# Storing each output tile of a fused attention and maxout kernel with one transfer of 128 rows instead of two of 64

## The chip, the cores and the metric

The kernel runs on one core of a Trainium2 chip. The metric is device time in microseconds (us) of the whole program, as a median of several runs. A profile of one execution gives a span, from the first to the last instruction, about 2 us below the run's time. Ratios are the mean time of one kernel's fast runs over the mean of the other's in the same rounds, so they are not quite the ratio of the medians that are quoted.

The engines, by what they do in this kernel (instructions on the page of the kernel before): TensorE (PE, 4316) multiplies matrices, VectorE (DVE, 521) and ScalarE (ACT, 289) do elementwise work, GpSimd (POOL, 260) copies and starts loads, SyncE (SP) issues transfers, the only thing that its timeline shows. The bytes are moved by DMA engines, of which the page counts sixteen. A run counts as slow when it is over 1.5% above the fastest of the same kernel, otherwise as fast; only fast runs are compared.

## The reference

```python
# q, k, v: (8, 12, 448, 64) float32; w1, w2, w3, w_out: (768, 768) float32
scores = q @ k.T / sqrt(64);  m = max(scores);  e = exp(scores - m)
attn   = (e / (sum(e) + exp(-m) + 1e-9)) @ v           # per batch and head
x      = attn, heads side by side                      # (3584, 768)
h      = maximum(maximum(x @ w1, x @ w2), x @ w3)
out    = h @ w_out                                     # (3584, 768) float32
```

## The kernel before

Attention runs group by group (four heads of a batch), and the projections of batches already finished fill TensorE's time in between. Queries stand in an unusual order inside the kernel: a batch has seven blocks of 64 columns, and column x of block n is output row 7 x + order[n]. An output tile takes two blocks (128 columns of `hT`), so its 128 rows are two sets of 64 rows; inside a set the rows are seven apart. In the code and the profiles `stp` are the scores, `e` their exponentials, `xn` and `xT` the attention's result and its transpose, `p_i` one projection, `hT` the maximum of the three, `op_ps` the last product and `o_sb` its copy that is stored. Each set is stored by one transfer:

```python
    NW = DM // 2
    order = (0, 2, 4, 6, 1, 3, 5)

    def out_piece(bp, t, c, w, queues):
        # ... six matmuls into op_ps[:, 0:w], lhsT = 128 columns of hT ...
        nc.vector.tensor_scalar(out=o_sb[:, c : c + w], in0=op_ps[:, 0:w], ...)
        if queues is None:
            return
        for half in range(2):
            n = 2 * t + half
            b = 2 * bp + n // T
            rows = out[b * S : (b + 1) * S].rearrange("(p t) m -> t p m", t=T)[order[n % T]]
            queues[half].dma_start(
                out=rows[:, outs[1] : c + w], in_=o_sb[half * HP : half * HP + HP, outs[1] : c + w]
            )
        outs[1] = c + w
```

SP's queue also carries the transposes that feed TensorE: `QT` and `KT` for the scores of a group two iterations ahead, and `xT` for the projections:

```python
    def transpose_dma(i):
        for dst, nm, o in ((QT[i], "q", 4), (KT[i], "k", 0)):
            nc.sync.dma_start_transpose(...)     # [cut]

    def x_transpose_dma(i):
        nc.sync.dma_start_transpose(out=..., in_=...)     # [cut] xT <- xn
```

The softmax here doesn't subtract the row's maximum and nothing guards it: scores larger than these inputs give would overflow.

Of the kernel before, what the change touches and what calls it, by code (L numbers as in the profile page):

```python
# [21 lines left out]
def kernel(  # L22
# [13 lines left out]
    B, H, S, D = q.shape  # L36
    NTOK, DM = out.shape
    DFF = moe_w1.shape[1]
    NDC = DM // 128
    NFC = DFF // 128  # L40
# [5 lines left out]
    HP = 64  # L46
    T = S // HP
# [86 lines left out]
    for nm, src, eng in (("k", k, nc.sync), ("q", q, nc.scalar)):  # L134
# [10 lines left out]
            outs=[],  # L145
# [333 lines left out]
    outs = {}  # L479
# [23 lines left out]
    NW = DM // 2  # L503
    order = (0, 2, 4, 6, 1, 3, 5)

    def out_piece(bp, t, c, w, queues):

        if c == 0:
            outs[0] = out_pool.tile([128, DM], FP32, tag="o_sb", name="o_sb")
            outs[1] = 0  # L510
        o_sb = outs[0]
        op_ps = ps_b.tile([128, 512], FP32, tag="b", name="op_ps")
        for fc in range(NFC):
            nc.tensor.matmul(  # L514
                out=op_ps[:, 0:w],
                lhsT=hT[bp][:, fc, ts(t, 128)],
                rhs=wout_sb[:, fc, c : c + w],
                start=(fc == 0),
                stop=(fc == NFC - 1),
            )  # L520
        nc.vector.tensor_scalar(  # L521
            out=o_sb[:, c : c + w], in0=op_ps[:, 0:w], scalar1=1.0 / LAMBDA, scalar2=None,
            op0=ALU.mult,
        )
        if queues is None:
            return
        for half in range(2):
            n = 2 * t + half
            b = 2 * bp + n // T
            rows = out[b * S : (b + 1) * S].rearrange("(p t) m -> t p m", t=T)[order[n % T]]  # L530
            queues[half].dma_start(
                out=rows[:, outs[1] : c + w], in_=o_sb[half * HP : half * HP + HP, outs[1] : c + w]
            )
        outs[1] = c + w


    UP = NDC * (S + 6)
    pieces = []
# [7 lines left out]
    def add_out(b):  # L546
        sy, sc = nc.sync, nc.scalar
        for t in range(0, 3) if b % 2 == 0 else range(3, 7):
            cuts = [(0, NW, None), (NW, NW, (sy, sy))]
            if b == B - 1 and t == 6:  # L550
                cuts = [(0, NW, (sy, sy)), (NW, 256, (sc, sc)), (NW + 256, 128, (sy, sc))]
            for c, w, queues in cuts:
                pieces.append((out_piece, (b // 2, t, c, w, queues), NFC * (w + 6)))

    def add_batch(b):
        add_up(b, 0, S, [(i, fc) for fc in range(NFC) for i in range(3)])
        add_out(b)
# [120 lines left out]
    for i in range(3, NI):  # L678
# [6 lines left out]
        for vi, units in enumerate(visits):  # L685
            n = 3 * i + vi
# [16 lines left out]
            if vi == 2 and first:  # L703
                x_transpose_pe(i - 1, "E")
                fill(per / 2)
                prep_v(i, DV)
                for w, cols in ((0, (0, NE)), (1, (0, NE)), (2, (NE, NO)), (2, (0, NE))):
                    add_up(0, *cols, [(w, f) for f in (0, 2, 4)])
                add_out(0)
                per = share(n)  # L710
# [59 lines left out]
```

## Time and profile before

| | before |
|---|---|
| median | 339.16 us (338.11 to 339.39, 4 runs) |
| span of the profile | 336.9 us |
| TensorE busy | 326.1 us, 97% |
| last VectorE work to the end | 331.9 to 336.9: 5.0 us |
| transfers for the stores | 60 (57 from SP, 3 from ACT), 11.01 MB |

The prediction below shows and reads the main lines. Two more are needed later: the count of DMA packets on the page, and the line of the waits for GpSimd's copies of QT (engine, line, whom it waited for, total us, times, longest).

```profile
DMA packets 84815, 46.46 MB, mean 138 GB/s; under 512 B 53280, under 2 KB 81312, under 8 KB 84768
...
POOL QT L249 <- DMA QT<-ld_q: 69.2, 11, 10.0
```

The packet count includes packets of 4 bytes, called semaphore packets here: 2656 of them on the queues of SP and ScalarE. A store of this kernel leaves sixteen (pair_one below has 30 stores fewer and exactly 480 such packets fewer), so the sixty stores make 960. I read it as one for each DMA engine that carries the store; the number of store packets in flight at a time, which in this kernel is sixteen for longer than any other number (10.3 of 53.5 us), agrees. This count will tell how many engines a transfer used.

### The profile page before, as it was taken

To read this page: it belongs to the slowest core of one execution; us is meant where nothing else is said; L and a number is where in the kernel's file an instruction comes from. 1 tells how busy PE (TensorE), PEld (TensorE's weight loads), DVE (VectorE), ACT (ScalarE), POOL (GpSimd) and SP (SyncE) were. 2 spreads that over 40 slices of the span, in tenths; PEclk is the share of its full clock that TensorE was granted. 3 is DMA by queue.
4 is the path that set the end of the run, shared out by engine and by line. 5 is a ranking of instruction groups with operands and counts; after the bars stand their busy time and mean duration, and the time that the engine had idled before them with its cause. 6 is when DMAs were issued, how large, how long until landed. Compare 5 with 4: busy or idle time off the path is not lost.

```text
span 336.9 us, 10248 instructions
## 1 busy us (share of the span) xinstructions
PE 326.1 (97%) x4316; PEld 195.9 (58%) x4316; DVE 199.9 (59%) x521; ACT 183.1 (54%) x289; POOL 146.7 (44%) x260
## 2 busy tenths in 40 slices
PE   7899999999999999999999999999999999999993
PEld 3668788866556655565546646555556555565552
DVE  4556675566566556556656556556556556575552
ACT  4768856655665755676556655666565665420000
POOL 8596578880671539170854328351754000000000
PEclk9999999999999999999999999999999999999999
DMA  8999999799799999969996999989990730124016
GB/s 141 197 200 207 203 205 191 128 161 191 109 108 132 171 234 145 124 96 190 177 156 81 114 259 120 150 99 220 186 149 18 164 89 2 31 47 129 0 33 157
DMA packets 84815, 46.46 MB, mean 138 GB/s; under 512 B 53280, under 2 KB 81312, under 8 KB 84768
## 3 DMA queue, kind: packets, MB, share of 16 engines
q0 software_dynamic: 29120, 21.80, 48.6%
q1 hardware_dynamic: 55264, 23.60, 41.3%
q8 instruction: 34, 0.56, 0.7%
q10 hardware_dynamic: 384, 0.39, 0.4%
q14 instruction: 13, 0.11, 0.1%
HBM read 44.04 MB, written 11.01 MB: 163 GB/s over the span
## 4 chain that ended last, share of the span: by engine, by line
PE 87%; DMA 5%; ACT 2%; DVE 2%; issue 1%; POOL 1%; POOLq 0%; ACTq 0%
PE p_i L490 48%; PE op_ps L514 14%; PE stp L304 11%; PE avp L388 9%; DMA xT<-xn 3%; ACT e L324 2%; DMA ld_q<-in_q_dram 2%; PE avp L344 2%; PE avp L361 1%; DVE xn L404 1%; PE trT L229 1%; DVE QT L190 1%; PE xtp L463 0%; ACT QT L188 0%; DVE rb L401 0%
## 5 line engine op out<-in xcount | busy, mean ns | idle before, releaser
L324 ACT ACTIVATE e<-stp 128x896 f16<-128x896 f32 (+4 forms) x171 | 143.9, 901 | 60.3 <-PE stp L304 60.1
L490 PE MATMUL p_i<-xT,w 128*128 128x448 f16 (+2 forms) x972 | 173.1, 332 | 0.5 <-DMA xT<-xn 0.3
L490 PEld LDWEIGHTS <-w 128*128 128x128 f16 x972 | 90.2, 98 | 69.1 <-issue 6.0
L249 POOL COPY QT<-QT 64x384 f16<-64x384 f16 (+1 forms) x84 | 46.9, 558 | 93.9 <-DMA QT<-ld_q 69.2
L501 DVE TENSOR_TENSOR hT<-hT,p_i 128x448 f16<-128x448 f16 (+2 forms) x96 | 59.7, 622 | 35.7 <-PE p_i L490 35.6
L514 PE MATMUL op_ps<-w,hT 128*128 128x384 f16 (+2 forms) x342 | 58.5, 323 | 0.0
L304 PE MATMUL stp<-QT,KT 64*64 64x448 f16 (+2 forms) x756 | 48.1, 338 | 2.6 <-ACT e L324 0.9
L499 DVE CAST hT<-p_i 128x448 f16<-128x448 f32 (+2 forms) x48 | 30.0, 625 | 25.2 <-PE p_i L490 25.2
L514 PEld LDWEIGHTS <-hT 128*128 128x128 f16 x342 | 32.0, 98 | 22.4 <-issue 2.0
L424 ACT ACTIVATE xn<-end,rl 64x64 f16<-64x64 f32 x72 | 24.9, 346 | 34.5 <-DVE rl L421 34.1
L521 DVE TENSOR_SCALAR o_sb<-op_ps 128x384 f32<-128x384 f32 (+2 forms) x57 | 31.2, 547 | 17.4 <-PE op_ps L514 16.8
L388 PE MATMUL avp<-vx,e 128*128 128x65 f16 x936 | 38.6, 194 | 0.0
L388 PEld LDWEIGHTS <-e 128*128 128x128 f16 x936 | 32.1, 97 | 2.3
L304 PEld LDWEIGHTS <-KT 64*64 64x64 f16 x756 | 15.8, 105 | 26.8 <-issue 23.9
L398 DVE TENSOR_SCALAR rb<-avp 128x6 f32<-128x6 f32 (+2 forms) x54 | 8.8, 164 | 36.8 <-PE avp L388 36.8
L404 DVE TENSOR_TENSOR xn<-avp,rb 128x384 f16<-128x384 f32 (+2 forms) x54 | 29.3, 543 | 1.8
L433 POOL COPY vx<-ld_v 128x768 f16<-128x768 f16 x21 | 17.2, 820 | 6.8 <-issue 4.2
L344 PEld LDWEIGHTS <-e 64*64 64x64 f16 x624 | 13.7, 107 | 8.1 <-issue 1.7
L102 POOL DMA_DIRECT2D ld_q<-in_q_dram x24 | 17.4, 723 | 2.3 <-DMA w<-in_moe_w_dram 1.1
L102 POOL DMA_DIRECT2D ld_k<-in_k_dram x24 | 17.3, 722 | 2.1 <-DMA w<-in_moe_w_out_dram 1.1
L414 ACT ACTIVATE end<-avp 128x65 f32<-128x65 f32 x36 | 8.2, 227 | 17.1 <-PE p_i L490 12.4
L115 POOL DMA_DIRECT2D ld_v<-in_v_dram x24 | 15.2, 634 | 2.6 <-DMA w<-in_moe_w_dram 1.3
(52 smaller groups left out, 162.1 us busy)
## 6 DMA issues: line engine op xcount, KB each, us to landing
out_dram<-o_sb SPq DMA_DIRECT2D x54, 192.0 KB, 4.0
ld_v<-in_v_dram POOLq DMA_DIRECT2D x48, 128.0 KB, 5.1
ld_k<-in_k_dram POOLq DMA_DIRECT2D x23, 224.0 KB, 6.6
ld_q<-in_q_dram POOLq DMA_DIRECT2D x23, 224.0 KB, 7.5
w<-in_moe_w_dram POOLq DMA_DIRECT2D x9, 384.0 KB, 9.2
w<-in_moe_w_out_dram POOLq DMA_DIRECT2D x3, 384.0 KB, 8.5
xT<-xn SPq DMA_TRANSPOSE x18, 4.8
QT<-ld_q SPq DMA_TRANSPOSE x17, 7.3
```

The costliest lines, as they stand in the source:

```text
L102: nc.gpsimd.dma_start(out=tiles[nm][:, 1 : NP * T + 1].rearrange("x (r t) d -> x r (t d)", r=NP)[:, p0:p1], in_=src[:, p0:p1],)
L249: eng.tensor_copy(out=t[d0 : d0 + HP, o * 128 : (o + n) * 128], in_=t[s0 : s0 + HP, a * 128 : (a + n) * 128],)
L304: nc.tensor.matmul(out=stp[half * HP : half * HP + HP, par, j * qn : (j + 1) * qn], lhsT=k_block(i, pr, h2, x[half]), rhs=q_cols(i, pr, h2 ...
L324: nc.scalar.activation(out=dst, in_=src, func=AF.Exp, scale=scale)
L388: nc.tensor.matmul(out=ps[:, hh, j * D1 : (j + 1) * D1], lhsT=eF[:, o : o + 128], rhs=vx[:, 2 * pr + hh, (x[0]), 0:D1], start=False, stop= ...
L404: nc.vector.tensor_tensor(out=xn[i][:, pr, ws[0] : ws[0] + nw].rearrange("p j h d -> p h j d"), in0=acc[:, :, :, 0:D], in1=rb.unsqueeze(3) ...
L424: nc.scalar.activation(out=xn[i][0:HP, pr, 3, hh], in_=end[h, 0:D], func=AF.Copy, scale=rl[h])
L490: nc.tensor.matmul(out=p_i[:, j * qn : (j + 1) * qn], lhsT=w_sb[i][:, dc, ts(fc, 128)], rhs=xT[b][:, dc, q0 : q0 + qn], start=(dc == 0), s ...
L499: nc.vector.tensor_copy(out=dst, in_=src)
L501: nc.vector.tensor_tensor(out=dst, in0=dst, in1=src, op=ALU.max)
L514: nc.tensor.matmul(out=op_ps[:, 0:w], lhsT=hT[bp][:, fc, ts(t, 128)], rhs=wout_sb[:, fc, c : c + w], start=(fc == 0), stop=(fc == NFC - 1),)
L521: nc.vector.tensor_scalar(out=o_sb[:, c : c + w], in0=op_ps[:, 0:w], scalar1=1.0 / LAMBDA, scalar2=None, op0=ALU.mult,)
```

## The change

The intent is fewer transfers: both sets of rows of a tile in one. It builds a pattern of three dimensions in DRAM by hand: 2 sets, 64 rows, the columns. Where the second set comes before the first in DRAM (t = 5, four tiles of 28) two transfers stay.

```diff
-        for half in range(2):
-            n = 2 * t + half
-            b = 2 * bp + n // T
-            rows = out[b * S : (b + 1) * S].rearrange("(p t) m -> t p m", t=T)[order[n % T]]
-            queues[half].dma_start(
-                out=rows[:, outs[1] : c + w], in_=o_sb[half * HP : half * HP + HP, outs[1] : c + w]
-            )
+        r0, r1 = ((2 * bp + n // T) * S + order[n % T] for n in (2 * t, 2 * t + 1))
+        cols = slice(outs[1], c + w)
+        for p0, r, k in ((0, r0, 2),) if r1 > r0 else ((0, r0, 1), (HP, r1, 1)):
+            at = out[r : r + 1, cols]
+            rows = bass.AP(
+                at.tensor, at.offset, [[abs(r1 - r0) * DM, k], [T * DM, HP], [1, c + w - outs[1]]]
+            )
+            queue.dma_start(out=rows, in_=o_sb[p0 : p0 + k * HP, cols])
...
-            cuts = [(0, NW, None), (NW, NW, (sy, sy))]
+            cuts = [(0, NW, None), (NW, NW, sy)]
             if b == B - 1 and t == 6:
-                cuts = [(0, NW, (sy, sy)), (NW, 256, (sc, sc)), (NW + 256, 128, (sy, sc))]
+                cuts = [(0, NW, sy), (NW, 256, sc), (NW + 256, 128, sy)]
```

More of the change, by code (lines that the diff above doesn't have):

```diff
@@ L504, with out_piece @@
     order = (0, 2, 4, 6, 1, 3, 5)
-    def out_piece(bp, t, c, w, queues):
+    def out_piece(bp, t, c, w, queue):
         if c == 0:
@@ L524, in out_piece @@
         )
-        if queues is None:
+        if queue is None:
             return
-        for half in range(2):
-            n = 2 * t + half
-            b = 2 * bp + n // T
-            rows = out[b * S : (b + 1) * S].rearrange("(p t) m -> t p m", t=T)[order[n % T]]
-            queues[half].dma_start(
-                out=rows[:, outs[1] : c + w], in_=o_sb[half * HP : half * HP + HP, outs[1] : c + w]
+        r0, r1 = ((2 * bp + n // T) * S + order[n % T] for n in (2 * t, 2 * t + 1))
[4 more added lines that the diff above has]
+                at.tensor, at.offset, [[abs(r1 - r0) * DM, k], [T * DM, HP], [1, c + w - outs[1]]]
             )
+            queue.dma_start(out=rows, in_=o_sb[p0 : p0 + k * HP, cols])
         outs[1] = c + w
@@ L548, in add_out @@
         for t in range(0, 3) if b % 2 == 0 else range(3, 7):
-            cuts = [(0, NW, None), (NW, NW, (sy, sy))]
+            cuts = [(0, NW, None), (NW, NW, sy)]
             if b == B - 1 and t == 6:
-                cuts = [(0, NW, (sy, sy)), (NW, 256, (sc, sc)), (NW + 256, 128, (sy, sc))]
-            for c, w, queues in cuts:
-                pieces.append((out_piece, (b // 2, t, c, w, queues), NFC * (w + 6)))
+                cuts = [(0, NW, sy), (NW, 256, sc), (NW + 256, 128, sy)]
+            for c, w, queue in cuts:
+                pieces.append((out_piece, (b // 2, t, c, w, queue), NFC * (w + 6)))
     def add_batch(b):
```

## The prediction

In this text k is the number of DMA engines that carry a transfer. k = 2 in the forecast is an assumption, as are that all merged stores use the same two engines and that loads and transposes spread evenly over sixteen. 339.3 + 37 + 17.7, less 0 to 1, came to 393, and was moved to 400; but the 37 and the 17.7 rest on k = 2.

> **What bounds the kernel now.** I read the page from the top: busy shares first, then the chain that ended last, then the DMA issues, then the stretch at the end of the span, then the DMA queue of SP.
>
> ```profile
> span 336.9 us, 10248 instructions
> PE 326.1 (97%) x4316; PEld 195.9 (58%) x4316; DVE 199.9 (59%) x521; ACT 183.1 (54%) x289; POOL 146.7 (44%) x260
> DMA  8999999799799999969996999989990730124016
> q0 software_dynamic: 29120, 21.80, 48.6%
> q1 hardware_dynamic: 55264, 23.60, 41.3%
> PE 87%; DMA 5%; ACT 2%; DVE 2%; issue 1%; POOL 1%; POOLq 0%; ACTq 0%
> ```
>
> TensorE is busy 97% of the span, and the chain that ended last is 87% TensorE. So a store matters only where TensorE waits for something behind it, and after TensorE's last work. But the DMA row is nearly as full as the PE row: q0 (loads) plus q1 (transposes and stores) take 90% of sixteen engines' time. [...] these shares overstate the use (single stretches of 10 us show 1.3 and more), but the DMA engines have no large reserve. The issues that matter:
>
> ```profile
> out_dram<-o_sb SPq DMA_DIRECT2D x54, 192.0 KB, 4.0
> xT<-xn SPq DMA_TRANSPOSE x18, 4.8
> QT<-ld_q SPq DMA_TRANSPOSE x17, 7.3
> ```
>
> A store of 64 rows lands in 4.0 us, and SP issues it on the same queue as the transposes that feed TensorE (QT and KT for the scores, xT for the projections). One batch of that queue, and TensorE's answer to it, in the timeline:
>
> ```profile
> 185.38 1.24 SPq L473 DMA_TRANSPOSE xT<-xn  x1
> 186.71 4.20 SPq L531 DMA_DIRECT2D out_dram<-o_sb  x6
> 191.07 1.98 SPq L241 DMA_TRANSPOSE QT<-ld_q  x1
> 194.98 2.95 SPq L241 DMA_TRANSPOSE KT<-ld_k  x1
> 198.02 1.18 SPq L531 DMA_DIRECT2D out_dram<-o_sb  x2
> ...
> 223.91 1.55 SPq L473 DMA_TRANSPOSE xT<-xn  x1
> 194.95 2.81 PE L490 MATMUL p_i<-xT,w 128*128 128x448 f16 x14 [0.29 <-DMA xT<-xn]
> ```
>
> The last transpose of a batch (185.38) is needed by TensorE at about 194.7, some 9 us later; here it came 0.29 us late. There is little slack for it, and stores sit on both sides of it. At the end of the span:
>
> ```profile
> 326.20 7.78 SPq L531 DMA_DIRECT2D out_dram<-o_sb  x9
> 330.49 1.43 DVE L521 TENSOR_SCALAR o_sb<-op_ps 128x384 f32<-128x384 f32 x3 [0.42 <-DMA out_dram<-o_sb]
> 331.60 1.84 ACTq L531 DMA_DIRECT2D out_dram<-o_sb  x3
> ```
>
> VectorE's last work ends at 331.9, and the remaining 5.0 us up to 336.9 are issuing and landing of the last stores: exposed. The last packet in the trace's packet records ends at 334.9, so 2.0 us follow it.
>
> [...]
> (1) [...] SP spends 0.47 and 0.59 us on the two issues at 326.20 and 326.72.
> (2) [...] I looked at the built programs. Before: 64 x 768 on both sides[...]. After: 2 x 64 x 768 in DRAM against 128 partitions. [...] The trace of before has no transfer of such a shape, so it can't confirm it.
> [...]
> (4) [...] an undisturbed packet of 3072 bytes takes 121 ns, 25.4 GB/s (two that overlap take about 240 each). I use 121 ns.
>
> **The change, part by part.** The instructions on TensorE, VectorE, ScalarE's compute and GpSimd stay in the same order; only store issues differ.
> - Removed: of 28 tiles (eight batches, 3.5 each) 24 become one transfer per column cut. Four tiles (t = 5, where the second row comes before the first) keep two. SP has 57 store issues before and 31 after; at some 0.55 us each that is 14 us of sequencer time, none of it on TensorE's path save about 1 us at the end. Worth at most 1 us.
> - Added, if k = 2: a merged tile puts 64 packets of 3072 bytes on each of two engines in place of 8 on each of sixteen. 64 x 0.121 = 7.7 us for a tile, where 8 x 0.121 = 1.0 us was enough. Landing goes from 4.0 to about 10 us on a quiet queue.
>
> The end. From the first of the last stores' packets (327.3) the two engines get: two full tiles 15.5 us; the split tile 8 packets, 1.0; the last tile's three cuts with 64 packets each of 1536 bytes (about 65 ns, 4.2), 1024 bytes (46 ns, 2.9) and 512 bytes (27 ns, 1.7). Sum 25.3 us, so the last packet ends at 352.6; plus 2.0 is 354.6 against 336.9: **+17.7 us**, all exposed. (The three stores before, from 301.5 on, take 23 us and are just done by 327.)
>
> The middle. Work of one of the two engines for one batch, by median packet times: loads per group are 16 packets of 896 bytes for k, as many for q (88 ns), 32 of 512 bytes for v (60 ns), 4.7 us, times 3 groups 14.2. Transposes: 22 blocks a group, each 128 packets over 16 engines, times 3 groups, 528 packets at 18 ns, 9.5. Stores 3.5 x 8 x 0.121 = 3.4. Together 27.1 us in a batch of 38.2 (from the xT issues at 147.37 and 261.91, three batches apart): it fits. After: three merged tiles and half a split one, 196 packets, 23.7 in place of 3.4: **47.4 us in 38.2**. The two engines become the bound, and each batch is longer by 9.2 us: the transposes come late and TensorE waits. Five batch intervals (70 to 262) have loads, transposes and stores together; the first starts with slack and the last has few loads left, so I count four: **+37 us**. Batch 5's stores (from 263) have 38 us in which few transposes follow, so I count nothing there.
> Sum: 339.3 + 37 + 17.7 - 0 to 1 = 393. The mean packet times, which contain contention (transposes 32 ns, loads 109 and 70, stores 156), would make the batch work 65 us and the middle over 100; service times must be nearer the medians, as the means count overlap twice. I move a little toward them: **400 us**.
>
> **The rivals.**
> - The shape does not limit the engines (k stays 16[...]). Then the bytes move as before, and only issues fall away: the end gains up to 1 us, the middle nothing as TensorE is full. 338.5 us, within 2%. For it: the old transfers all used 16, and no row of this trace shows k below. [...] I give it 10%.
> - k = 2, but the middle hides it: six o_sb buffers and a lead of two groups for QT and KT soak up the backlog, and only the end shows: 339.3 + 17.7 = 357 us. Against: 47.4 us of work do not fit into 38.2 however they are buffered, and the xT transpose has some 9 us of slack.
> - Worse than the sum: behind each burst the QT and KT transposes come late, then the xT ones, and the two engines idle while TensorE catches up, so that waits add instead of overlapping; or packets take their contended times. A batch of 55 to 60 us gives about 430 to 450 us.
> - Faster by over 2%: it would take 7 us, more than the exposed end of 5.0 us holds. Next to impossible.
>
> **Range and chances.** Below lies "end only" at 357, above the contended case at 450: a range of 358 to 455. Faster 1%, within 2% 10%, slower 89%.
>
> **What would show it.** Right: the landing of the merged stores is 10 us or more in the middle of the page's DMA issues; xT, QT and KT land later than 4.8 and 7 us, and TensorE's idle time before p_i L490 and stp L304 is released by these DMAs (before: 0.3 us), about 9 us a batch; TensorE's share falls to some 82%; the gap from the last VectorE work to the end is about 23 us instead of 5.0. The packet count stays near 84,800 and packets of 3072 bytes stay about 121 ns. Wrong: merged stores that land in 4 to 5 us mean that k is 16; waits that appear only at the end mean that the middle hid it; 3072-byte packets much shorter than 121 ns, or a batch that grows by far more or less than 9 us while the end is as computed, mean that my sum of engine work is off.

## The result, and the profile after

The changed kernel takes 416.1 us (415.09 to 417.28, 4 runs) against 339.16 us: ratio 1.2277, 95% interval 1.2234 to 1.2321. It is slower by 77 us and inside the predicted range.

The page of the changed kernel (span; busy time by engine; TensorE's granted clock in tenths, in 40 slices; DMA packets; then the chain that ended last):

```profile
span 414.7 us, 10220 instructions
PE 337.3 (81%) x4316; PEld 200.3 (48%) x4316; DVE 199.8 (48%) x521; ACT 183.1 (44%) x289; POOL 146.4 (35%) x260
PEclk9999999998995899999689995899957999999955
DMA packets 84034, 46.45 MB, mean 112 GB/s; under 512 B 52500, under 2 KB 80532, under 8 KB 83988
...
PE 50%; DMA 23%; SPq 8%; POOL 6%; ACT 3%; DVE 2%; issue 2%; POOLq 0%; ACTq 0%
```

The instruction counts of VectorE, ScalarE and GpSimd and their busy times are the same as before within 0.3 us. TensorE's share has fallen to 81%, and the chain is no longer TensorE's: DMA and SP's issuing (SPq) hold 31% of it. There are 781 packets fewer, with the same bytes.

That number identifies what happened. The changed kernel has 34 store transfers: 26 merged ones and 8 of 64 rows. With two engines for a merged one the semaphore packets are 26 x 2 + 8 x 16 = 180 in place of 960, so 780 fewer. The packet records have 1876 in place of 2656, exactly 780 fewer; the one left over belongs to a different queue. On sixteen engines throughout it would have been 34 x 16 = 544, so 416 fewer. The records also show how many packets of 3072 bytes are in flight: mostly two at a time, in 156 of the 202 us in which any runs, where before sixteen is the commonest number.

The middle of the run, SP's queue in the timeline over one batch (start us, duration us of issuing):

```profile
217.30 1.26 SPq L473 DMA_TRANSPOSE xT<-xn  x1
218.66 14.10 SPq L534 DMA_DIRECT2D out_dram<-o_sb  x4
232.93 8.22 SPq L241 DMA_TRANSPOSE QT<-ld_q  x1
241.24 2.84 SPq L241 DMA_TRANSPOSE KT<-ld_k  x1
...
269.12 2.50 SPq L473 DMA_TRANSPOSE xT<-xn  x1
```

It answers to the batch from 185.38 to 223.91 shown of before. The batch takes 51.8 us in place of 38.5. Four stores, two of them merged, take 14.1 us just to issue where six took 4.2, and the transpose of QT behind them takes another 8.2 us to issue. These long issues fall into the time in which earlier stores still run. (The longest issue of one transpose in this kernel is 17.16 us, at 78.24 behind three merged stores; the shortest take 1.2.) The trace's packet records show the engines' side: from 223.1 to 256.1 store packets of 3072 bytes run with one pause, of 3 us. There are 20 to 34 of them in 2 us (more only around 233, up to 80, where the tile of two transfers is stored), and 34 is two engines with one packet in about 118 ns each. The 256-byte packets of transposes stop for up to 11.7 us at a time meanwhile; in the kernel before their longest pause between 69 and 262 us is 8.0.

What waits for that, from the view of waits (total us, times, longest):

```profile
POOL QT L249 <- DMA QT<-ld_q: 120.0, 8, 22.3
...
PE stp L304 <- DMA KT<-ld_k: 30.8, 3, 12.2
...
PE p_i L490 <- DMA xT<-xn: 15.8, 2, 13.1
```

GpSimd's shifted copies of QT wait 120 us in place of 69.2, the scores wait 30.8 us for KT, and the projections wait 15.8 us for xT in place of 0.3. Here is such a wait in TensorE's timeline, with what follows it:

```profile
204.66 0.96 PE L304 MATMUL stp<-QT,KT 64*64 64x448 f16 x8 [8.02 <-DMA KT<-ld_k]
...
206.92 5.22 PE L490 MATMUL p_i<-xT,w 128*128 128x448 f16 x18
```

The same 18 matmuls in the kernel before:

```profile
177.56 3.57 PE L490 MATMUL p_i<-xT,w 128*128 128x448 f16 x18
```

After 8 us of idleness these matmuls run slower for a few microseconds, and the clock row above has slices at 5 to 8 tenths where that of before has 9 throughout. In this trace TensorE is idle from 196.6 to 204.6, the granted clock is 0.50 in each of the five microseconds from 204.6 to 209.6 and 1.00 from 210.6 on, and the first of these matmuls start 373 ns apart, the last 189. The clock came back some 5.6 us after the work did. I had not counted it.

The end of the run, in the timeline (SP's last stores, VectorE's last work):

```profile
386.76 19.23 SPq L534 DMA_DIRECT2D out_dram<-o_sb  x6
391.05 1.44 DVE L521 TENSOR_SCALAR o_sb<-op_ps 128x384 f32<-128x384 f32 x3 [0.42 <-PE op_ps L514]
```

VectorE ends at 392.5, and the span at 414.7: 22.2 us in place of 5.0.

So the 77.8 us of span split into two. The end grew by 22.2 - 5.0 = 17.2 us. The rest, 60.6 us, is how much later VectorE's last work ends (392.49 against 331.92). For TensorE this middle is 49.4 us of idle time and 11.2 us of longer matmuls: busy time went from 326.1 to 337.3, and idle time up to its last matmul from 336.9 - 326.1 - 5.3 = 5.5 to 414.7 - 337.3 - 22.5 = 54.9, where 5.3 and 22.5 follow the last matmul. Of the idle time after the change 46.6 us are the two waits shown, for KT and for xT.

### The profile page after: what moved, and what is told of

Same layout as the page of the kernel before. It is cut to its first block, busy times and chain, and to the rows that moved or that the text cites. A ratio compares the mean times of both kernels' runs of the same rounds, so it can differ in the third digit from the quotient of the medians.

```text
span 414.7 us, 10220 instructions
## 1 busy us (share of the span) xinstructions
PE 337.3 (81%) x4316; PEld 200.3 (48%) x4316; DVE 199.8 (48%) x521; ACT 183.1 (44%) x289; POOL 146.4 (35%) x260
## 4 chain that ended last, share of the span: by engine, by line
PE 50%; DMA 23%; SPq 8%; POOL 6%; ACT 3%; DVE 2%; issue 2%; POOLq 0%; ACTq 0%
PE p_i L490 24%; DMA QT<-ld_q 14%; PE op_ps L514 10%; DMA KT<-ld_k 8%; SPq L241 7%; PE stp L304 6%; PE avp L388 5%; DMA ld_q<-in_q_dram 2%; ACT e L324 2%; POOL QT L249 2%; SPq L534 1%; PE warm L175 1%; PE avp L344 1%; POOL ld_k L102 1%; POOL ld_v L112 1%
## 5 line engine op out<-in xcount | busy, mean ns | idle before, releaser
L490 PE MATMUL p_i<-xT,w 128*128 128x448 f16 (+2 forms) x972 | 180.7, 341 | 17.8 <-DMA xT<-xn 15.8
L490 PEld LDWEIGHTS <-w 128*128 128x128 f16 x972 | 92.3, 100 | 92.0 <-issue 32.6
L304 PE MATMUL stp<-QT,KT 64*64 64x448 f16 (+2 forms) x756 | 49.5, 345 | 35.0 <-DMA KT<-ld_k 30.8
L388 PE MATMUL avp<-vx,e 128*128 128x65 f16 x936 | 39.9, 197 | 0.0
L521 DVE TENSOR_SCALAR o_sb<-op_ps 128x384 f32<-128x384 f32 (+2 forms) x57 | 31.2, 547 | 17.4 <-PE op_ps L514 17.2
L388 PEld LDWEIGHTS <-e 128*128 128x128 f16 x936 | 33.3, 99 | 2.4
L433 POOL COPY vx<-ld_v 128x768 f16<-128x768 f16 x21 | 17.2, 818 | 3.1 <-DMA ld_v<-in_v_dram 2.1
```

The costliest lines, as they stand in the source:

```text
L304: nc.tensor.matmul(out=stp[half * HP : half * HP + HP, par, j * qn : (j + 1) * qn], lhsT=k_block(i, pr, h2, x[half]), rhs=q_cols(i, pr, h2 ...
L388: nc.tensor.matmul(out=ps[:, hh, j * D1 : (j + 1) * D1], lhsT=eF[:, o : o + 128], rhs=vx[:, 2 * pr + hh, (x[0]), 0:D1], start=False, stop= ...
L490: nc.tensor.matmul(out=p_i[:, j * qn : (j + 1) * qn], lhsT=w_sb[i][:, dc, ts(fc, 128)], rhs=xT[b][:, dc, q0 : q0 + qn], start=(dc == 0), s ...
```

## The experiments

Theory A: the number of DMA engines is the cause. A merged store, whose hand-built pattern has an outermost dimension of 2 in DRAM, runs on two engines, as counted above, and they are overloaded. Rival B: the merging is the cause, one large transfer in place of two small ones. Further questions were how much of the middle is the sum of the two engines' work, and how much is waiting behind stores in SP's queue.

### Which of the two: engines or merging

**split62**, the kernel before with nothing merged, each half cut into 62 and 2 rows. I expected two engines for each of these, and the count and the packets in flight below show two:

```diff
-            queues[half].dma_start(out=rows[:, ...], in_=o_sb[half * HP : half * HP + HP, ...])
+            for p0, m in ((0, HP),) if t == 5 else ((0, 62), (62, 2)):
+                queues[half].dma_start(out=rows[p0 : p0 + m, ...], in_=o_sb[half * HP + p0 : half * HP + p0 + m, ...])
```

> The kernel before with nothing merged: each half of a tile (64 rows) goes as 62 and 2 rows[...]; t = 5 stays at 64 rows as in the changed kernel. Theory A (number of engines): 64 packets of 3072 bytes on each of two engines for a tile, exactly as in the changed kernel, so 408 to 428 us and an end of about 22 us after VectorE. Rival B (merging, the larger transfer, is the cause): 339 to 345 us.

Measured: 419.9 us, ratio 1.2354 (1.2255 to 1.2454), result correct. Transfers are at most half the size and more than three times as many as in the changed kernel, and the time is nearly the same. Its timeline at the end:

```profile
387.18 24.24 SPq L532 DMA_DIRECT2D out_dram<-o_sb  x16
...
391.47 1.44 DVE L521 TENSOR_SCALAR o_sb<-op_ps 128x384 f32<-128x384 f32 x3 [0.42 <-PE op_ps L514]
```

From VectorE's end (392.91) to the end of the span (416.3) are 23.4 us. Rival B is refuted: without any merging the loss is there.

**pair_one and pair_two** merge without confining. Block n of two consecutive batches is put side by side in `hT`; the 128 rows of a tile then have one constant distance in DRAM (64 x 7 = 448 rows is just one batch), so the pattern is 128 x 768:

```diff
-        dst = hT[b // 2][:, fcs[0] : fcs[0] + len(fcs), o : o + qn]
+        blk = hT[b // 2][:, fcs[0] : fcs[0] + len(fcs), :].rearrange("p f (n h x) -> p f n h x", h=2, x=HP)
+        dst = blk[:, :, q0 // HP : (q0 + qn) // HP, b % 2]
...
+        rows = out[bp * 2 * S : (bp + 1) * 2 * S].rearrange("(p t) m -> t p m", t=T)[order[t]]
+        for p0, n in ((0, P),):        # pair_two: ((0, HP), (HP, HP)); pair_k4: ((0, 124), (124, 4))
+            queue.dma_start(out=rows[p0 : p0 + n, cols], in_=o_sb[p0 : p0 + n, cols])
...
-        for t in range(0, 3) if b % 2 == 0 else range(3, 7):
+        for t in range(0, 0) if b % 2 == 0 else range(0, 7):
```

> Block n of two batches side by side in hT (runs of 64 elements stay contiguous for VectorE), so a tile's 128 rows have one constant stride in DRAM: one transfer, k = 16. All seven tiles of a pair now follow the odd batch, which takes filler work from the last attention groups. Theory A: near the kernel before plus what that order costs, 338 to 352 us, and stores land in 3 to 5 us. Rival B: above 390.

> Control for pair_one: same order and layout, two transfers of 64 rows. Theory A: pair_one and this within 1.5 us of each other, this one the slower if at all (one more issue at the end). Rival B: pair_one slower by 50 us or more.

Measured: pair_one 340.24 us, ratio 1.0018 (0.9935 to 1.0102); pair_two 341.03 us, ratio 1.0029 (0.9962 to 1.0097). Both are correct and equal to the kernel before within the noise. The merged stores of pair_one on its page:

```profile
DMA packets 84335, 46.45 MB, mean 138 GB/s; under 512 B 52801, under 2 KB 80833, under 8 KB 84289
...
out_dram<-o_sb SPq DMA_DIRECT2D x27, 384.0 KB, 4.0
```

A transfer of 384 KB lands in 4.0 us here, as one of 192 KB did in the kernel before; so it is not the size of the merged transfers that made the changed kernel slow. Merging itself is worth 0.8 us here by the medians, which is not clear of the noise: the runs of pair_one (339.32 to 341.45) span those of pair_two (340.93 to 341.13). In the two profiles the time from VectorE's end to the span's end is 3.4 us in pair_one and 5.2 in pair_two. Against the kernel before that gain is lost again: VectorE ends at 334.1 in place of 331.9, which I put down to the changed order (all seven tiles after the odd batch).

### How the loss depends on the number of engines

**contig_one, contig_two, contig_k2, contig_k4.** A first attempt at a constant distance: VectorE writes `hT` in the order of the output rows, so a tile is 128 rows that follow each other.

```diff
+        whole = hT[b // 2][:, fcs[0] : ..., (b % 2) * S : (b % 2 + 1) * S].rearrange("p f (x t) -> p f t x", t=T)
+        for n0, n, t0 in parts:        # blocks 0-3 are rows 0,2,4,6 of seven, blocks 4-6 rows 1,3,5
+            to, frm = whole[:, :, t0 : t0 + 2 * n - 1 : 2], src[:, :, n0 : n0 + n]
+            ...                        # copy or maximum, as before
+        r = bp * 2 * S + t * P
+        for p0, n in ((0, P),):        # two: 64+64; k2: 122+6; k4: 124+4 rows
+            queue.dma_start(out=out[r + p0 : r + p0 + n, cols], in_=o_sb[p0 : p0 + n, cols])
```

> The columns of hT are put in the order of the output rows, so each of the 28 tiles is 128 rows that follow each other in DRAM: one transfer, 128 x 768 on both sides, k = 16. The price is one more VectorE instruction for each full-width p_i piece (about 150 ns each, some 110 times, VectorE at 59% before). Theory A (the two-engine shape is the cause): 337 to 342 us, stores land in 4 to 5 us, TensorE above 95%. Rival B (one large transfer in place of two small ones is the cause, whatever its shape): near 416 us, above 390. A 2% loss to 346 would be VectorE's strided writes and not the stores.

> Control for contig_one: the same hT order and VectorE work, each tile stored as two transfers of 64 rows. Theory A: within 1 us of contig_one (at most 1 us slower, from the issues at the end). Rival B: near the kernel before, far faster than contig_one. The difference to contig_one is what the merging itself is worth.

> As contig_two, but the tile is cut into 122 and 6 rows[...]. Same bytes, as many transfers as contig_two, nothing merged. Theory A: a tile is 62 packets on each of two engines, end +23.5 us (31.1 us of packets from 327.3), a batch of some 50 to 54 us: 420 to 445 us. Rival B (merging is the cause): as contig_two, near 340.

> The tile cut into 124 and 4 rows[...]. Theory A: 32 packets of 121 ns on each of four engines, 3.9 us a tile; a batch of engine work 37.3 us in 38.2, so the middle almost fits (0 to 15 us lost); end 16.0 us of packets from 327.3, +8.4 us: 347 to 363 us in all. Rival B: as contig_two, near 340. A rival in which the loss of the middle is all or nothing (any confined store delays the transposes in full): above 390.

Measured: contig_one 417.02 us, contig_two 419.01, contig_k2 459.15 and contig_k4 429.6 us (the last two with two runs each). Of these contig_one, contig_k2 and contig_k4 miss their expectations in absolute time, and contig_two is 2.0 us from contig_one where at most 1 was expected. The first misses by 75 us, and by coincidence equals the changed kernel. Taken alone it would have spoken for Rival B. Its chain and its group of maxima (busy us, mean ns) tell otherwise:

```profile
DVE 55%; PE 39%; issue 2%; DMA 1%; ACT 1%; POOL 0%; POOLq 0%; ACTq 0%
...
L506 DVE TENSOR_TENSOR hT<-hT,p_i 128x256 f16<-128x256 f16 (+3 forms) x180 | 181.3, 1242 | 3.2 <-PE p_i L491 3.1
```

VectorE has become the bound, at 360.5 us busy in place of 199.9. Its writes now step 14 bytes from element to element: a full-width maximum takes an instruction of 256 columns (1280 ns) and one of 192 (1100 ns) in place of one of 448 (622 ns); the casts, which only write `hT`, take 1240 and 1086 ns in place of 625. I had expected about 150 ns more. The runs show the cost, not the mechanism. The control contig_two has the same VectorE work with unmerged stores and is no faster, so merging costs nothing here either: contig_one gains 2.0 us on it, and its stores of 384 KB land in 2.9 us.

The four kernels remain comparable with each other. Against contig_two, contig_k4 loses 10.6 us, nearly all of it at the end (15.6 us from VectorE's end to the span's end in place of 5.3). Its batches take longer because of VectorE, and 37 us of engine work, the estimate from packet times, fit into them. contig_k2 loses 40.1 us, with 28.0 us at the end. It has as many transfers as contig_two and merges nothing, so neither the merging nor the number of issues can be the cause of its loss.

**pair_k4**, four engines in the pair kernel:

> As pair_one, tile cut into 124 and 4 rows: 4 engines. Theory A, engine work per batch 37.3 us in 38.2: the end +8.4 us over pair_two, the middle 0 to 20 us more as bursts of seven tiles take 27 us of four engines' time; 8 to 28 us over pair_two. Rival B: equal to pair_two.

Measured: 382.92 us in its one fast run (the other, 391.06 us, was slow, and the profile is of that one). The loss over pair_two is 42 us, above the expected 8 to 28. Two parts of the expectation were wrong. In this order all seven tiles come at the end, not four, so the end costs more: 21.1 us in place of 5.2 in that profile. And if the end is as long in the fast run, the middle loses some 26 us although the sum of engine work, 37.3 us in a batch of 38.2, just fits. Its stores come in bursts of seven tiles, 27 us of work for each of four engines. I take it that the transposes wait behind the burst longer than their lead lasts, but no run isolates that.

**The count of engines in all these kernels.** The second column has the engines that I expected for each transfer; it is the semaphore packets that show them. They agree to the packet:

| kernel | store transfers and engines | semaphore packets with these | fewer than 960 | fewer packets on the page |
|---|---|---|---|---|
| changed | 26 x 2, 8 x 16 | 180 | 780 | 781 |
| split62 | 104 x 2, 8 x 16 | 336 | 624 | 624 |
| pair_one | 30 x 16 | 480 | 480 | 480 |
| pair_k4 (124 + 4 rows) | 30 x 4, 30 x 4 | 240 | 720 | 720 |
| contig_k2 (122 + 6 rows) | 30 x 2, 30 x 6 | 240 | 720 | 719 |
| last_batch_only | 48 x 16, 5 x 2, 2 x 16 | 810 | 150 | 150 |

The last column is 84,815 minus the kernel's packet count. Where it is one off, the 4-byte packets alone are not: in the packet records of these six kernels they are fewer by exactly the number in the column before it. The count gives only the sum over a tile's two transfers, which is 8 engines for 122 + 6 rows and for 124 + 4 rows alike. The packets of 3072 bytes in flight tell these apart: mostly two at a time in contig_k2 (171 us) and split62 (156 us), four in contig_k4 (93 us) and pair_k4 (90 us).

### The end and the middle apart

**last_batch_only:** the merged stores for the last four tiles alone.

```diff
-        for p0, r, k in ((0, r0, 2),) if r1 > r0 else ((0, r0, 1), (HP, r1, 1)):
+        for p0, r, k in ((0, r0, 2),) if r1 > r0 and bp == 3 and t >= 3 else ((0, r0, 1), (HP, r1, 1)):
```

> The merged two-engine stores only for the last batch (four tiles), two transfers of 64 rows everywhere else. Theory A with the sum of the prediction: only the exposed end grows, by 17 us, so 354 to 359 us, and the last VectorE work still ends near 332 us. If a merged store costs something beyond its place (for instance in every wait of SP), it is more.

Measured: 356.55 us, ratio 1.0522 (1.0456 to 1.0588). VectorE ends at 331.2, the span at 353.7: 22.5 us.

```profile
329.81 1.43 DVE L521 TENSOR_SCALAR o_sb<-op_ps 128x384 f32<-128x384 f32 x3 [0.42 <-PE op_ps L514]
```

The end is a separate loss of 17 us, as the sum of packet times said, and these merged stores cost nothing before it.

**half_cols:** the changed kernel, but only columns 0 to 383 are stored, so the result is wrong.

```diff
-        cols = slice(outs[1], c + w)
+        cols = slice(0, NW)
+        if bp == B // 2 - 1 and t == 6 and c > 0:
+            return
```

> Wrong result on purpose: the changed kernel, but each store takes only columns 0 to 383, so 64 packets of 1536 bytes (65 ns) on each of two engines, 4.2 us a tile. By the sum of the prediction a batch is then 36.6 us of engine work in 38.2 and fits. Capacity alone: the middle loses 0 to 10 us, the end 5 to 6 us, 344 to 356 us. Waiting behind the bursts (transposes queue behind two or three stores whatever the sum): a good part of the 60 us of the middle stays, 370 to 400 us.

Measured: 342.57 us, ratio 1.0081 (1.0046 to 1.0116). From its page and its timeline:

```profile
PE 326.6 (96%) x4316; PEld 196.3 (58%) x4316; DVE 199.0 (58%) x521; ACT 183.0 (54%) x289; POOL 146.5 (43%) x260
```

```profile
330.13 1.44 DVE L521 TENSOR_SCALAR o_sb<-op_ps 128x384 f32<-128x384 f32 x3 [0.42 <-PE op_ps L514]
```

VectorE ends at 331.6, before the 331.9 of the kernel before, though each merged store still has the shape that ran on two engines in the changed kernel, and goes from SP's queue ahead of the same transposes. The whole middle loss is gone once a tile takes the two engines 4.2 us in place of 7.7 (the estimates 64 x 65 ns and 64 x 121 ns). The end keeps 9.1 us, 4.1 more than before. So stores of this shape are harmless in the middle when a batch's work on them is 36.6 us and a burst of three or four tiles takes 13 to 17 (3 or 4 times 4.2). This kernel lowers the sum and the length of the bursts at once, so it does not tell which of the two the middle's loss hangs on; pair_k4, whose sum fits and whose bursts are long, suggests that the bursts count too.

**act_k2 and act_k16:** stores issued by ScalarE, so that they don't share a queue with the transposes.

```diff
-            cuts = [(0, NW, None), (NW, NW, sy)]
+            cuts = [(0, NW, None), (NW, NW, sc)]          # act_k16: (sc, sc), in the kernel before
```

> The changed kernel with its stores issued by ScalarE instead of SP, so that transposes no longer stand behind stores in one queue; still two engines. Capacity alone: the two engines have the same 47 us a batch, so 390 us or more. Waiting behind stores in the queue: the transposes overtake, up to six tiles of stores pile up in the o_sb buffers, 350 to 380 us. A confusion to look for: issues that block ScalarE, which must also compute the exponentials.

> Control for act_k2: the kernel before with its stores issued by ScalarE, 16 engines. 337 to 346 us; what it loses is the cost of issuing from ScalarE.

Measured: act_k2 437.96 us, ratio 1.2878 (1.2813 to 1.2943); act_k16 345.89 us in its fast run (355.84 in a slow one). Separate queues did not help: the loss over the control is larger than that of the changed kernel. The packets of the transposes do get through better, with a longest pause of 7.8 us between 69 and 330 us, where the changed kernel has 12.2. But SP, whose queue holds no stores until the last tile, still takes long to issue them:

```profile
221.84 10.68 SPq L241 DMA_TRANSPOSE QT<-ld_q  x1
```

So long issues need no store ahead in the same queue. The time agrees with capacity, but it does not prove it, because the feared confusion is there. In act_k2's waits of ScalarE:

```profile
ACT e L324 <- issue: 22.0, 5, 8.2
```

ScalarE's exponentials stood still for 22 us in five places, up to 8.2 us, for no reason that the profile names. I take it that its own stores held up its sequencer: their issues, three of them taking 8.68 us at 222.81 for instance, are as long as SP's, and the exponentials go on at 231.54, right after those three. How much order in the queue matters when the engines are overloaded is left open.

## Why the prediction was right or wrong

**k = 2: right.** The semaphore packets count it exactly (180 in place of 960), and split62, contig_k2 and pair_one show that the number of engines is the cause, and merging is not. The runs show the count, not why it is two.

**Cost of a tile, 64 x 121 ns: right.** The median packet of 3072 bytes took 121 ns before and after, and two were in flight at a time.

**The end, +17.7 us: right.** It measured +17.2 us in the changed kernel and VectorE's end to the span's end is the same in last_batch_only to 0.3 us.

**Removed issues, up to 1 us: right in kind, and not had in the changed kernel.** A gain shows only where the merged store keeps sixteen engines: 2.0 us in the contig kernels, whose merged stores have the 128 x 768 shape that pair_one counts at sixteen, 0.8 within the noise in the pair kernels, and an end that is 1.8 us shorter in the profile of pair_one than in that of pair_two. In the changed kernel issuing got slower. The prediction also counts 31 issues from SP after the change; the page has 33 (23, 9 and 1), which makes its 14 us of sequencer time 13 and changes nothing else.

**The middle, +37 us: right in mechanism, too small.** It measured 60.6 us. The step that was mis-sized is "each batch is longer by 9.2 us", counted four times. The four intervals from the xT issue at 116.57 to that at 322.74 are 51.5 us each in place of 37.9 (110.27 to 261.91 in the kernel before): +13.6 and not +9.2. The first interval, counted as nothing, lost 6.3 us (116.57 against 110.27). Together that is 60.8 us, the whole loss of the middle. The sum of 47.4 us is 4.1 us short of the measured batch, and the runs do not settle what fills the rest. Three things were left out of the sum:
- It assumed that the two engines never rest. In the batch from 217.3 to 269.1 no store packet runs before 223.1 or after 256.1, and the two engines have nothing but loads and transposes there, 19 us. The next tile only exists once TensorE has its transposes, and those came late. Part of the prediction's third rival, waits that add instead of overlapping, may thus be in it. This is read from the packets, which do not name their engine, and not shown by an experiment: the prediction has 23.7 us of loads and transposes for these engines in a batch, which can fill such a stretch.
- It took median packet times. Between 116.57 and 322.74 the mean of a 3072-byte packet is 134.8 ns; if that is what it cost the engine, the 196 packets take 2.7 us more than the 23.7 counted (an estimate).
- TensorE was busy 11.2 us longer, with a mean granted clock of 0.910 in place of 0.999; it fell after a wait, as shown above. How much of that reached the end is not known, because TensorE can be slower without a loss where it would have waited for DMA anyway.

The condition itself, that the loss comes when the work exceeds the batch, agrees with half_cols, which at 36.6 us in 38.2 lost nothing in the middle. But pair_k4 lost some 26 us there with a sum that fits, so the sum alone does not decide: how the loss divides between too much work and waits behind long bursts stays open.

**The last step, from 393 to 400: luck.** No sum stands behind it. It went the right way, but its reason was packets that take their contended times, and the mean of the 3072-byte packets fell from 156 to 142 ns.

**The rivals.** "End only" (357 us) is what last_batch_only does at 356.6; in the changed kernel the buffers could not absorb the overload. "k stays 16" (338.5 us) is what pair_one does, at 340.2.

**What would show it.** TensorE's share (82% said, 81% measured) and the last gap (23 us said, 22.2 measured) came out. TensorE's waits for xT and KT came out too: 46.6 us together, some 9 for each of five batches. The landing of the merged stores could not be read: the page gives none for them, nor for the transposes after the change. The packet count, which I had expected unchanged, was the better witness. None of the experiments beats the kernel before beyond the noise.

## What to carry to other kernels

Before two transfers are merged by a hand-built access pattern, look at its outermost dimension, because in the kernels here the number of DMA engines that carried the bytes went with it: 16 at 128 and at 64 rows, 4 at 124, 2 at 122 and at 62, and 2 for two sets of 64, by the count of semaphore packets together with the packets in flight. An outer dimension of 2 cost 77 us, where fewer issues gained 2 at most. Count a transfer's work per engine and add it to what else that engine must do in the same stage: here it was harmless while the sum fitted and the bursts were short (half_cols, 36.6 us in 38.2 by the estimate from packet times), and where the sum did not fit (47.4 us in 38.2) it became the bound of a kernel that had looked bound by TensorE. If rows can be laid out at one constant distance by choosing what goes side by side in a tile, the merged store keeps all engines (pair_one, sixteen semaphore packets a store), but check what the new layout does to the engine that writes the tile: in contig_one VectorE was busy 360.5 us in place of 199.9.
